# A fixed order for VectorE and ScalarE in the last stage of a fused kernel, block sums kept in DRAM, and the last tile product by product

## The chip, the cores and the metric

The kernel runs on one core of one Trainium2 chip. The metric is the device time of one execution in microseconds. Before the change it is 856.98 us, the median of three runs (856.64, 856.98 and 858.51).

## The reference

Windowed attention feeds two feed-forward blocks. The weights (w1, w2, w3, both w_out, w_in) are 64-bit floats, q, k and v are 32-bit, and the output is 32-bit.

```python
# attention: batch 4, heads 8, sequence 576, head size 64, window 64
scores = (q @ k.T) / 8, masked to 0 <= i - j < 64
x = softmax(scores) @ v                      # reshaped to 2304 tokens x 512
# first block: 512 -> 1024 -> 512
y = ((x @ w1) * (x @ w2)) @ w3 @ w_out
# second block: 512 -> 2048 -> 512
h = y @ w_in
g = maximum(0.01 * h, h)
out = (g @ w_out2).astype(float32)
```

## The kernel before, in words

Every matrix product is made of three products of split operands (`mm3`, lines 74 to 77): an operand is cut into a high part (a ScalarE copy to fp32r) and a low part (a VectorE subtraction), and high x high, high x low and low x high are added up in PSUM. So each operand tile costs one ScalarE and one VectorE pass before TensorE can use it; this is called a split below. 64-bit weights are loaded as words and made into 32-bit floats by integer operations (scale, shift, sign).

The work has four stages.

1. Weight words are loaded and converted, w3 and w_out are multiplied into one matrix, and the attention of batch 0 runs.
2. For each batch, `ab_step` and `y_step` compute (x w1)(x w2) and its product with w3 w_out, and store y to the DRAM tensor `yd`. The attention of the next batch and the words of w_in are woven in. In this attention p, the softmax result, is transposed by a store to DRAM (`pd`, line 213) and four loads back (`pts`, line 216).
3. h = y w_in by seven products of half-size blocks in place of eight (a Strassen form): 24 `Quad`s, one for each pair of column blocks p (0 to 7) and token group c (0 to 2), each of seven products of six matmuls. One product is one slot. `prepare(t)` runs what is planned for slot t: splits of y and w_in blocks with the sums that the form needs (`y_parts`, `w_parts`), the conversion of w_out2 words (`c_load`, `c_scale`, `c_shift`, `c_sign`, which end with a store to `wd`), and the first preparations of the last stage. h goes to DRAM (`hd`). c11, c21, c22, c12 (tiles `c`) collect the products; a ScalarE copy keeps a product, a VectorE add joins another (line 651).
4. out = g w_out2, again by seven products. A step is (g, k): a token group g of 512 tokens (the fifth has 256) and a pair k of blocks of w_out2, eight k to a group. For each step `h_load` fetches h, `h_sums` applies the leaky ReLU on ScalarE (line 814) and makes block sums on VectorE (lines 817 to 819), `h_split` makes the operand (lines 828 and 829), and `o_quad` runs 21 matmuls for each tile of 128 rows: two tiles to a step, one in group five. The operand of w_out2, one unit for each k, is made once by `v_load` (two loads from `wd`) and `v_parts`: four sums (line 788) and four splits (lines 791 and 792). After k = 7 `o_out` adds the seven products of a tile (lines 858 and 860) and stores two pieces of the output.

What sets the order: a scheduler places the instructions of each engine in a list before the run, from the program order, priorities (`first()`), and `tc.issue_after(x)`, which puts an instruction behind x in its list. At run time each engine works its list in order. DMAs issued by SyncE stand in one such list (SP) too. Pools with a number of buffers (raw 4, f 4, io 2, c 8) make a load or an operation wait until a buffer's last reader is done. The eight PSUM banks of the last stage (`ps3`) take the place of the eight of the stage before, and one tile of the output uses four of them through its eight k.

The order of the last stage before is this loop (line 974 on), whose instructions the scheduler may move against one another:

```python
h_load(i + 4); h_sums(i + 3)
for q in range(width(i) // P):
    o_quad(i, q)
h_split(i + 2)
if i < len(later): ...   # units 5 to 7 of w_out2
```

Of the kernel before, what the change touches and what calls it, by code (L numbers as in the profile page):

```python
# [21 lines left out]
def tile_kernel(ctx: ExitStack, tc: tile.TileContext, q, k, v, w1, w2, w3, w_out, w_in, w_out2, out):  # L22
# [62 lines left out]
    wd = dram.tile([2 * KF2, P, UC], F32, name="wd")  # L85

# [120 lines left out]
    def tp(g):  # L207
# [372 lines left out]
    def w_parts(p):  # L580
# [179 lines left out]
    def c_sign(f):  # L760
        u = conv.pop(f)
        g = u["f"].bitcast(I32)
        dve.scalar_tensor_tensor(out=g, in0=u["hi"], scalar=-0x80000000, in1=g, op0=ALU.bitwise_and, op1=ALU.bitwise_or)
        sp.dma_start(wd[KF2 + f], u["f"])

    vin, vop = {}, {}

    def v_load(k):
        vin[k] = stage.tile([P, 2, 2, 2 * P], F32, name="raw", tag="raw", bufs=RAW)
        for h in range(2):  # L770
            sp.dma_start(vin[k][:, h].rearrange("p c m -> p (c m)"), wd[KF2 + 2 * k + h])

    def v_parts(k, tile):

        own = {}

        def part(j):
            if j == 0:
                vop[k] = tile()
            u, t = vin[k], vop[k]  # L780
            a11, a21, a12, a22 = u[:, 0, 0], u[:, 0, 1], u[:, 1, 0], u[:, 1, 1]
            if j == 1:
                own["sums"] = [stage.tile([P, 2, 2 * P], F32, name="io", tag="io", bufs=2) for _ in range(2)]
            if j in (1, 2):
                s1, s2, s3, s4 = (own["sums"][i // 2][:, i % 2] for i in range(4))
                for o, x0, x1, op in (((s1, a21, a22, ALU.add), (s2, s1, a11, ALU.subtract)),
                                      ((s3, a11, a21, ALU.subtract), (s4, a12, s2, ALU.subtract)))[j - 1]:
                    dve.tensor_tensor(out=o, in0=x0, in1=x1, op=op)
            for at, x in (((0, u[:, 0, 0:1]), (1, u[:, 1])), ((3, own.get("sums", (0,))[0]),), ((5, own.get("sums", (0, 0))[-1]),))[j]:
                w = slice(at, at + x.shape[1])  # L790
                act.copy(t[:, 0, w], x)
                dve.tensor_tensor(out=t[:, 1, w], in0=x, in1=f32(t[:, 0, w]), op=ALU.subtract)
# [17 lines left out]
    def h_sums(i):  # L810

        if i < len(steps):
            x = hin[i]
            act.activation(out=x, in_=x, func=AF.Prelu, alpha=0.01)
            x = hin[i] = x.rearrange("p f (t m) -> p (f t) m", t=2)
            t13, t24 = hsum[i] = [stage.tile([P, 2, width(i)], F32, name="f", tag="f", bufs=4) for _ in range(2)]
            dve.tensor_tensor(out=t13, in0=x[:, 1:4:2], in1=x[:, 0:2], op=ALU.subtract)
            dve.tensor_tensor(out=t24[:, 0], in0=x[:, 3], in1=t13[:, 0], op=ALU.subtract)
            dve.tensor_tensor(out=t24[:, 1], in0=x[:, 2], in1=t24[:, 0], op=ALU.subtract)

    def h_split(i):

        if i < len(steps):
            x, (t13, t24) = hin.pop(i), hsum.pop(i)
            u = g_units[i % len(g_units)] if len(g_units) == 3 else g_units[i]
            for at, y in ((0, x[:, 0:1]), (1, x[:, 2:4]), (3, t13), (5, t24)):
                h, l = (u[:, n, at:at + y.shape[1], 0:width(i)] for n in range(2))
                act.copy(h, y)  # L828
                dve.tensor_tensor(out=l, in0=y, in1=f32(h), op=ALU.subtract)  # L829
# [3 lines left out]
    def o_quad(i, q):  # L833

        g, k = steps[i]
        w, y = vop[k], g_units[i % 3]
        ts = slice(P * q, P * q + P)
        if k == 0:
            po[g, q] = [ps3.tile([P, 2, 2 * P], F32, name="o") for _ in BANKS]
        for bank, ms in enumerate(BANKS):  # L840
            for n, m in enumerate(ms):
                a, b = O_PRODUCTS[m]
                with tc.issue_after(pss["pr"]):
                    pss["pr"] = mm3(po[g, q][bank][:, n], y[:, 0, b, ts], y[:, 1, b, ts], w[:, 0, a], w[:, 1, a],
                                    k == 0 and n == 0, k == NF - 1, True)
# [174 lines left out]
```

## Time and profile before

| | before |
|---|---|
| median of three runs | 856.98 us |
| the profiled execution | 859.36 us |
| its span, first to last instruction | 857.6 us |
| TensorE matmul busy | 806.6 us, 94% |
| VectorE busy | 583.9 us, 68% |
| ScalarE busy | 446.6 us, 52% |
| mean granted TensorE clock | 0.986 of full speed |

Busy shares are means over four unlike stages. What a change of one stage can be worth is read from TensorE's idle time and granted clock in that stage, and from what ended the idle time. Stage three runs from about 475 to 657 us of the span, stage four from there to the end.

### The profile page before, as it was taken

What the parts mean: (1) busy time and instruction counts of PE and PEld (TensorE: products, weight loads), DVE (VectorE), ACT (ScalarE), POOL (GpSimd) and SP (SyncE); (2) the same over time, 40 slices, a digit from 0 to 9 for tenths busy, and PEclk for the clock granted to TensorE, in tenths of its full rate; (3) what the DMA queues carried; (4) which work ended last, traced back from release to release, by engine and by line L of the source; (5) the groups of instructions that cost most, each with busy time, mean ns of one, the idle gap of its engine ahead of it and who ended that gap; (6) DMA issues with size and microseconds to landing.
All of it is one profiled execution on the core that took longest, in us unless ns stands there. A gap on an engine that the chain in (4) does not pass through costs nothing.

```text
span 857.6 us, 16756 instructions
## 1 busy us (share of the span) xinstructions
PE 806.6 (94%) x5980; PEld 774.5 (90%) x5980; DVE 583.9 (68%) x1505; ACT 446.6 (52%) x1095; POOL 66.4 (8%) x77
## 2 busy tenths in 40 slices
PE   5689799999999999898999999999998989999997
PEld 3567698999999999898999989999998988999997
DVE  6799896663655367665821765866569997788875
ACT  6687883432434244343521654655457675656543
POOL 1012553110111011110000000000000000000000
PEclk9999999999999999999999999999999999999999
DMA  7798688664545537667510346888756444343321
GB/s 244 202 221 221 190 213 203 145 145 89 126 109 135 114 98 179 181 182 236 182 46 2 111 157 233 296 286 278 246 184 203 133 150 131 115 144 104 124 86 63
DMA packets 200755, 139.52 MB, mean 163 GB/s; under 512 B 136416, under 2 KB 170720, under 8 KB 200672
## 3 DMA queue, kind: packets, MB, share of 16 engines
q1 hardware_dynamic: 196064, 133.74, 54.5%
q10 hardware_dynamic: 4608, 4.72, 1.7%
q8 instruction: 47, 0.77, 0.4%
q14 instruction: 36, 0.29, 0.1%
HBM read 94.63 MB, written 43.78 MB: 161 GB/s over the span
## 4 chain that ended last, share of the span: by engine, by line
PE 72%; DMA 10%; DVE 9%; ACT 3%; SPq 2%; issue 2%; POOL 0%; DVEq 0%; ACTq 0%; POOLq 0%
PE o L75 7%; PE o L77 7%; PE o L76 7%; PE ab L75 7%; PE ab L77 6%; PE ab L76 6%; PE pr L77 6%; PE pr L75 6%; PE pr L76 6%; PE mm L75 4%; DMA raw<-in_moe_w_dram 4%; PE mm L76 4%; PE mm L77 3%; PE sc L175 3%; PE pa L229 2%
## 5 line engine op out<-in xcount | busy, mean ns | idle before, releaser
L75 PE MATMUL ab<-x,w 128*128 128x288 f32 x512 | 154.2, 302 | 6.0 <-ACT x L235 2.8
L77 PE MATMUL ab<-x,w 128*128 128x288 f32 x512 | 152.1, 297 | 0.0
L76 PE MATMUL ab<-x,w 128*128 128x288 f32 x512 | 152.1, 297 | 0.0
L77 PE MATMUL pr<-yop,w 128*128 128x384 f32 x300 | 102.0, 340 | 2.5 <-DVE w L598 2.5
L75 PEld LDWEIGHTS ab<-x,w 128*128 128x128 f32 x512 | 97.2, 190 | 7.7 <-ACT x L235 2.9
L75 PE MATMUL pr<-yop,w 128*128 128x384 f32 x300 | 101.7, 339 | 0.0
L76 PE MATMUL pr<-yop,w 128*128 128x384 f32 x300 | 101.5, 338 | 0.0
L77 PEld LDWEIGHTS ab<-x,w 128*128 128x128 f32 x512 | 97.1, 190 | 0.1
L76 PEld LDWEIGHTS ab<-x,w 128*128 128x128 f32 x512 | 97.0, 190 | 0.1
L648 ACT COPY c<-pr 128x384 f32<-128x384 f32 x95 | 45.5, 479 | 67.1 <-PE pr L77 64.7
L75 PE MATMUL mm<-ab,wf 128*128 128x288 f32 x256 | 77.2, 313 | 2.1 <-ACT io L521 2.1
L75 PE MATMUL o<-yop,yop 128*128 128x256 f32 x259 | 74.4, 287 | 4.7 <-DVE res L858 3.0
L77 PE MATMUL mm<-ab,wf 128*128 128x288 f32 x256 | 74.8, 294 | 0.0
L76 PE MATMUL mm<-ab,wf 128*128 128x288 f32 x256 | 74.7, 294 | 0.0
L77 PE MATMUL o<-yop,yop 128*128 128x256 f32 x259 | 73.6, 284 | 0.0
L76 PE MATMUL o<-yop,yop 128*128 128x256 f32 x259 | 73.5, 284 | 0.0
L502 DVE TENSOR_TENSOR p<-ab,a 128x288 f32<-128x288 f32 x64 | 28.9, 452 | 60.5 <-PE ab L77 59.9
L651 DVE TENSOR_TENSOR c<-pr,c 128x384 f32<-128x384 f32 x74 | 41.1, 556 | 38.7 <-PE pr L77 22.0
L183 ACT ACTIVATE s<-s,nm 128x128 f32<-128x128 f32 x144 | 56.6, 396 | 20.0 <-DVE nm L179 19.2
L497 ACT COPY a<-ab 128x288 f32<-128x288 f32 x64 | 25.4, 398 | 77.9 <-PE ab L77 75.4
L829 DVE TENSOR_TENSOR yop<-f,yop 128x512 fp32r<-128x512 f32 (+1 forms) x80 | 48.7, 636 | 25.0 <-ACT yop L828 23.8
L192 POOL TENSOR_TENSOR s<-s,rs 128x384 f32<-128x384 f32 x48 | 41.3, 861 | 297.1 <-DVE rs L191 200.9
(127 smaller groups left out, 2095.7 us busy)
## 6 DMA issues: line engine op xcount, KB each, us to landing
hd<-c SPq DMA_DIRECT2D x96, 192.0 KB, 2.6
raw<-in_moe_w_dram SPq DMA_DIRECT2D x32, 512.0 KB, 4.7
raw<-hd SPq DMA_DIRECT2D x32, 512.0 KB, 3.7
raw<-in_moe_w_out_dram SPq DMA_DIRECT2D x24, 512.0 KB, 4.5
raw<-in_moe_w_in_dram SPq DMA_DIRECT2D x16, 512.0 KB, 4.9
wd<-f SPq DMA_DIRECT2D x32, 256.0 KB, 4.3
raw<-wd SPq DMA_DIRECT2D x30, 256.0 KB, 4.0
vt<-in_v_dram SPq DMA_DIRECT2D x56, 128.0 KB, 2.9
```

Of the source, the lines that this page charges most:

```text
L75: pe.matmul(ps, lhsT=lh, rhs=rh, start=first, stop=False, skip_group_check=more)
L76: pe.matmul(ps, lhsT=lh, rhs=rl, start=False, stop=False, skip_group_check=more)
L77: return pe.matmul(ps, lhsT=ll, rhs=rh, start=False, stop=last, skip_group_check=more).ins
L175: pe.matmul(sc[:, t, :], lhsT=qb[:, t, :], rhs=kT[n][:, k0:k0 + P], start=True, stop=True)
L183: act.activation(out=s[:, t, :], in_=s[:, t, :], func=AF.Exp, bias=nm[:, t:t + 1], scale=-1.0, accum_out=sm[:, t:t + 1])
L192: pool.tensor_tensor(out=s, in0=s, in1=rs.unsqueeze(2).to_broadcast([P, GT, P]), op=ALU.mult)
L229: pe.matmul(o[W * h:W * h + W, W * t:W * t + W], lhsT=vt[:, a, h, m, :], rhs=pts[:, 2 * h:2 * h + 2, t], start=True, stop=True)
L497: pss["copy"] = act.copy(pss["a"], ps).ins
L502: dve.tensor_tensor(out=p32, in0=ps, in1=pss["a"], op=ALU.mult)
L648: pss["copy"] = act.copy(self.sb[to], ps).ins
L651: pss["add"] = dve.tensor_tensor(out=self.sb[to], in0=self.ps[at], in1=self.sb[of or to], op=ALU.add).ins
L829: dve.tensor_tensor(out=l, in0=y, in1=f32(h), op=ALU.subtract)
```

## The change

- **Words behind p's store.** The loads of w_in's words in the second stage were issued behind the last of p's loads back (`pss["store"]` set at line 216); now behind p's store.
- **Buffers of `w_parts`' sums.** They were in io; now in raw for p = 1 and 2, in io for p = 0, in f for the rest.
- **Block sums of w_out2 in DRAM.** The words are converted in pairs, every 11 slots, and the four sums of a pair are made right after (`c_sums`) and stored to a new DRAM tensor `vd`. `v_load` loads them (two loads more, into f or io), and `v_parts` has splits only.
- **Fixed order of the last stage.** Every VectorE operation of it is tied behind the one before it in the program (`two`), every ScalarE operation too (`copy`, `split`); the first ones come behind the last add and the last copy of stage three. The loop has h_split(i + 2), h_sums(i + 3), units of w_out2, the products, then `o_out`; in a step with k = 7 h_sums comes after `o_out`.
- **The last tile product by product.** The last two k of the last tile are joined: product m of k = 6, then product m of k = 7, then the next m. Its last store is cut in two halves of columns, one issued by ScalarE.

```diff
-        sp.dma_start(pd, tb)
+        pss["store"] = sp.dma_start(pd, tb).ins
...
-            pss["store"] = sp.dma_start(pts[32 * b:32 * b + 32], pd[:, b].rearrange("(a j) t i -> j a (t i)", a=4)).ins
+            sp.dma_start(pts[32 * b:32 * b + 32], pd[:, b].rearrange("(a j) t i -> j a (t i)", a=4))
...
             if j == 1:
-                own["sums"] = [stage.tile([P, 2, 2, P], F32, name="io", tag="io", bufs=2) for _ in range(2)]
+                if p in (1, 2):
+                    both = stage.tile([P, 2, 2, 2, P], F32, name="raw", tag="raw", bufs=RAW)
+                    own["sums"] = [both[:, 0], both[:, 1]]
+                else:
+                    tag, n = ("f", 4) if p else ("io", 2)
+                    own["sums"] = [stage.tile([P, 2, 2, P], F32, name=tag, tag=tag, bufs=n) for _ in range(2)]
...
+    def c_sums(k):
+        f0, f1 = (conv.pop(2 * k + h)["f"] for h in range(2))
+        a11, a21, a12, a22 = (f[:, 2 * P * c:2 * P * c + 2 * P] for f in (f0, f1) for c in range(2))
+        sums = [stage.tile([P, 2, 2 * P], F32, name="io", tag="io", bufs=2) for _ in range(2)]
+        s1, s2, s3, s4 = (sums[i // 2][:, i % 2] for i in range(4))
+        for o, x0, x1, op in ((s1, a21, a22, ALU.add), (s2, s1, a11, ALU.subtract), (s3, a11, a21, ALU.subtract),
+                              (s4, a12, s2, ALU.subtract)):
+            dve.tensor_tensor(out=o, in0=x0, in1=x1, op=op)
+        for i in range(2):
+            sp.dma_start(vd[k, i], sums[i].rearrange("p c m -> p (c m)"))
+
+    chain = {}
+
+    def tied(name, f):
+
+        with tc.issue_after(chain[name]) if name in chain else nullcontext():
+            chain[name] = f().ins
...
+    def split(t, at, x, n):
+        h, l = (t[:, i, at:at + x.shape[1], 0:n] for i in range(2))
+        copy(h, x)
+        two(l, x, f32(h))
...
+        for h in range(2):
+            sp.dma_start(vin[k][1 + h].rearrange("p c m -> p (c m)"), vd[k, h])
...
-            if j in (1, 2):
-                s1, s2, s3, s4 = (own["sums"][i // 2][:, i % 2] for i in range(4))
...
+            u, s12, s34 = vin[k]
+            for at, x in (((0, u[:, 0, 0:1]), (1, u[:, 1])), ((3, s12),), ((5, s34),))[j]:
+                split(vop[k], at, x, 2 * P)
...
-    for f in range(KF2):
-        t0 = 38 + 5 * f
-        for n, g in ((0, c_load), (7, c_scale), (8, c_shift), (9, c_sign)):
-            at_slot(t0 + n, lambda f=f, g=g: g(f))
+    for k in range(NF):
+        t0 = 38 + 11 * k
+        for n, g, h in ((0, c_load, 0), (0, c_load, 1), (7, c_scale, 0), (8, c_shift, 0), (8, c_scale, 1), (9, c_sign, 0),
+                        (9, c_shift, 1), (10, c_sign, 1)):
+            at_slot(t0 + n, lambda f=2 * k + h, g=g: g(f))
+        at_slot(t0 + 11, lambda k=k: c_sums(k))
...
+    end = [(len(GROUPS) - 1, NF - 2), (len(GROUPS) - 1, NF - 1)]
+    for i, (g, k) in enumerate(steps):
+        with tc.issue_after(pss["copy"]), tc.issue_after(pss["add"]):
+            if i == 0:
+                h_sums(2)
+            h_load(i + 4)
+            h_split(i + 2)
+            if k < NF - 1:
+                h_sums(i + 3)
+            if i < len(later):
+                if i in (2, 4):
+                    v_load(5 + i // 2)
+                run(later[i])
+            for q in range(width(i) // P):
+                if (g, k) not in end:
+                    o_quad(g, q, [k])
+                elif k == NF - 1:
+                    o_quad(g, q, [k - 1, k])
+                if k == NF - 1:
+                    o_out(g, q)
+            if k == NF - 1:
+                h_sums(i + 3)
```

The lists of the two kernels differ on VectorE at these places. The first is the start of stage three, in the list before: w_6153 is the operand of w_in block p = 2, io_6165 and io_6166 its sums, raw_6209 and yop1_6185 belong to y of token group 1, and the c rows are adds that join products.

```order
L593 TENSOR_TENSOR io_6165<-raw_5981 128x256
L550 TENSOR_TENSOR raw_6210<-f_6035,f_6031 128x384
L550 TENSOR_TENSOR raw_6209<-f_6035,raw_6209 128x384
...
L598 TENSOR_TENSOR w_6153<-io_6165,w_6153 128x512
L553 TENSOR_TENSOR yop1_6185<-f_6254,yop1_6185 128x384
L553 TENSOR_TENSOR yop1_6185<-raw_6210,yop1_6185 128x384
L651 TENSOR_TENSOR c_6309<-pr_6314,c_6309 128x384
L550 TENSOR_TENSOR raw_6297<-f_6252,f_6250 128x384
L550 TENSOR_TENSOR raw_6298<-f_6256,f_6252 128x384
L553 TENSOR_TENSOR yop1_6185<-f_6256,yop1_6185 128x384
L598 TENSOR_TENSOR w_6153<-io_6166,w_6153 128x512
```

The same place in the list after, where the sums of p = 2 are in raw_6165 (those of p = 1 stand 25 rows further up, ahead of the last products of stage two).

```order
L657 TENSOR_TENSOR c_6151<-pr_6156,c_6151 128x384
L599 TENSOR_TENSOR raw_6165<-raw_5982 128x256 x2
L604 TENSOR_TENSOR w_6153<-raw_5982,w_6153 128x256
L599 TENSOR_TENSOR raw_6165<-raw_6165,raw_5982 128x256
L599 TENSOR_TENSOR raw_6165<-raw_5982,raw_6165 128x256
L604 TENSOR_TENSOR w_6153<-raw_5982,w_6153 128x512
L554 TENSOR_TENSOR yop1_6184<-f_6030,yop1_6184 128x384
L554 TENSOR_TENSOR yop1_6184<-f_6034,yop1_6184 128x384
L604 TENSOR_TENSOR w_6153<-raw_6165,w_6153 128x512 x2
L657 TENSOR_TENSOR c_6202<-pr_6187,c_6202 128x384
```

In the whole lists six adds of stage three stand ahead of the last split of p = 2 before, and one after; y's rows come behind it now.

The second place is the end of stage three on VectorE, in the list before. c_8041 is the last add; raw_8073 and raw_8078 are h of the steps 2 and 3, and io_8018 a sum of w_out2's unit 4.

```order
L651 TENSOR_TENSOR c_8043<-pr_8009,c_8041 128x384
L651 TENSOR_TENSOR c_8002<-pr_8046,c_8002 128x384
L818 TENSOR_TENSOR f_8083<-raw_8073,f_8082 128x256
L817 TENSOR_TENSOR f_8090<-raw_8078 128x512
L788 TENSOR_TENSOR io_8018<-raw_7923,io_8017 128x256
L829 TENSOR_TENSOR yop2_8080<-raw_8073,yop2_8080 128x256
L651 TENSOR_TENSOR c_8041<-pr_8055,c_8041 128x384
```

After, with c_8094 as the last add and raw_8133 as h of step 2:

```order
L794 TENSOR_TENSOR w_8063<-f_7982,w_8063 128x512
L657 TENSOR_TENSOR c_8096<-pr_8068,c_8094 128x384
L657 TENSOR_TENSOR c_8061<-pr_8099,c_8061 128x384
L657 TENSOR_TENSOR c_8094<-pr_8108,c_8094 128x384
L794 TENSOR_TENSOR f_8139<-raw_8133 128x512
L794 TENSOR_TENSOR f_8140<-raw_8133,f_8139 128x256
```

The sums of steps 2 and 3 stood ahead of the last add and now stand behind it.

The third place is the end of the first token group on VectorE, in the list before. The o tiles are the PSUM banks that `o_out` reads (first tile o_8095 to o_8098), the yop and f rows are splits and sums of later steps.

```order
L829 TENSOR_TENSOR yop_7632<-raw_8424,yop_7632 128x512
L858 TENSOR_TENSOR res_8579<-o_8095,c_8580 128x256
L858 TENSOR_TENSOR c_8581<-o_8096,c_8580 128x256
L819 TENSOR_TENSOR f_8554<-raw_8492,f_8554 128x256
L818 TENSOR_TENSOR f_8638<-raw_8550,f_8637 128x256
L829 TENSOR_TENSOR yop1_7863<-raw_8492,yop1_7863 128x256
L858 TENSOR_TENSOR c_8582<-o_8096,c_8581 128x256
L858 TENSOR_TENSOR res_8613<-o_8120,c_8614 128x256
L858 TENSOR_TENSOR c_8615<-o_8121,c_8614 128x256
L819 TENSOR_TENSOR f_8638<-raw_8550,f_8638 128x256
L829 TENSOR_TENSOR yop1_7863<-f_8553,yop1_7863 128x512
L858 TENSOR_TENSOR c_8581<-o_8097,c_8581 128x256
```

After, with the first tile in o_8165 to o_8168:

```order
L794 TENSOR_TENSOR yop_7703<-f_8551,yop_7703 128x512
L794 TENSOR_TENSOR res_8628<-o_8165,c_8629 128x256
L794 TENSOR_TENSOR c_8630<-o_8166,c_8629 128x256
L794 TENSOR_TENSOR c_8631<-o_8166,c_8630 128x256
L794 TENSOR_TENSOR c_8630<-o_8167,c_8630 128x256
L794 TENSOR_TENSOR res_8628<-o_8167,c_8631 128x2x256
L794 TENSOR_TENSOR res_8628<-o_8168,c_8630 128x256
L794 TENSOR_TENSOR res_8662<-o_8190,c_8663 128x256
```

Splits and sums stood between the reads of the banks; now the six reads of a tile stand together.

## Rows read from the trace of the kernel before

**Rows 1.** The page, part 1: span.

```profile
span 857.6 us, 16756 instructions
```

**Rows 2.** Stretches: length; busy (instructions) of PE, PEld, DVE, ACT, POOL; clock; DMA share, GB/s.

```profile
485.00:500.00 15.00, 12.51 (x61) 11.54 (x60) 13.87 (x30) 8.69 (x19) 0.00 (x0) 0.89 0.59 190
500.00:657.30 157.30, 157.30 (x900) 156.99 (x899) 106.64 (x212) 87.96 (x180) 0.00 (x0) 1.00 0.72 242
657.30:667.00 9.70, 6.41 (x40) 6.21 (x40) 7.99 (x18) 5.90 (x10) 0.00 (x0) 0.82 0.59 183
...
680.00:700.00 20.00, 20.00 (x171) 20.00 (x170) 20.00 (x43) 14.31 (x25) 0.00 (x0) 1.00 0.50 160
...
702.00:715.00 13.00, 9.01 (x55) 8.06 (x54) 11.20 (x27) 6.72 (x12) 0.00 (x0) 0.87 0.48 162
...
751.50:756.00 4.50, 3.82 (x27) 3.05 (x26) 4.50 (x12) 1.14 (x3) 0.00 (x0) 1.00 0.63 189
...
798.00:852.84 54.84, 54.84 (x461) 54.63 (x459) 37.58 (x100) 27.24 (x63) 0.00 (x0) 1.00 0.25 78
```

**Rows 3.** Waits of PE from 474.8 us on: total us, times, longest.

```profile
PE pr L77 <- DVE w L598: 2.5, 2, 2.1
...
PE o L75 <- DVE res L858: 3.5, 4, 1.5
PE o L75 <- DVE c L651: 3.3, 2, 2.6
```

**Rows 4.** Timeline, start of stage three: start, length, operation, [idle before <- releaser].

```profile
480.79 0.43 DVE L593 TENSOR_TENSOR io<-raw 128x256 f32<-128x256 f32 x1 [1.39 <-ACT w L597]
...
495.84 0.69 DVE L598 TENSOR_TENSOR w<-io,w 128x512 fp32r<-128x512 f32 x1
...
496.58 0.69 PE L77 MATMUL pr<-yop,w 128*128 128x384 f32 x1 [2.08 <-DVE w L598]
```

**Rows 5.** Timeline, from stage three to four.

```profile
659.32 1.06 ACT L814 ACTIVATE raw<-raw 128x1024 f32<-128x1024 f32 x1 [3.58 <-DMA raw<-hd]
...
660.40 0.69 DVE L817 TENSOR_TENSOR f<-raw 128x512 f32<-128x512 f32 x1 [1.71 <-ACT raw L814]
...
661.68 0.55 DVE L651 TENSOR_TENSOR c<-pr,c 128x384 f32<-128x384 f32 x1
...
662.29 0.38 PE L75 MATMUL o<-yop 128*128 128x256 f32 x1 [2.65 <-DVE c L651]
```

**Rows 6.** One stretch, line 788 alone: length, DVE busy (instructions), clock, DMA.

```profile
641.00:695.00 54.00, 9.69 (x24) 0.97 0.51 161
```

**Rows 7.** Timeline, end of the second token group.

```profile
753.13 0.42 DVE L858 TENSOR_TENSOR res<-o,c 128x256 f32<-128x256 f32 x1
...
753.60 0.39 PE L75 MATMUL o<-yop,yop 128*128 128x256 f32 x1 [0.56 <-DVE res L858]
```

**Rows 8.** Timeline, the end.

```profile
852.56 0.28 PE L77 MATMUL o<-yop,yop 128*128 128x256 f32 x1
...
853.18 1.01 DVE L858 TENSOR_TENSOR res<-o,c 128x512 f32<-128x512 f32 x2
...
854.31 0.39 SPq L870 DMA_DIRECT2D out_dram<-res  x1
```

**Rows 9.** Timeline, p's round trip late in stage two.

```profile
385.51 0.42 SPq L213 DMA_DIRECT2D pd<-tb  x1
...
391.22 1.74 SPq L216 DMA_DIRECT2D pts<-pd  x4
...
394.67 0.57 PE L229 MATMUL pa<-pts,vt 128*64 128x64 f32 x12 [2.03 <-DMA pts<-pd]
```

**Rows 10.** DMA issues, 360 to 400 us, and whole page: count, KB, us to landing.

```profile
raw<-in_moe_w_in_dram SPq DMA_DIRECT2D x8, 512.0 KB, 4.8
...
pts<-pd SPq DMA_DIRECT2D x20, 48.0 KB, 1.9
...
wd<-f SPq DMA_DIRECT2D x32, 256.0 KB, 4.3
```

More of the change, by code (lines that the diff above doesn't have):

```diff
@@ L85, in tile_kernel @@
     wd = dram.tile([2 * KF2, P, UC], F32, name="wd")
+    vd = dram.tile([NF, 2, P, UC], F32, name="vd")
     stage = tc.alloc_tile_pool(name="stage", bufs=2, side="right")
@@ L764, in c_sign, with copy, two @@
         sp.dma_start(wd[KF2 + f], u["f"])
+    def c_sums(k):
[12 more added lines that the diff above has]
+            chain[name] = f().ins
+    def copy(out, x):
+        tied("act", lambda: act.copy(out, x))
+    def two(out, in0, in1, op=ALU.subtract):
+        tied("dve", lambda: dve.tensor_tensor(out=out, in0=in0, in1=in1, op=op))
+    def split(t, at, x, n):
+        h, l = (t[:, i, at:at + x.shape[1], 0:n] for i in range(2))
+        copy(h, x)
+        two(l, x, f32(h))
     vin, vop = {}, {}
     def v_load(k):
-        vin[k] = stage.tile([P, 2, 2, 2 * P], F32, name="raw", tag="raw", bufs=RAW)
+        tag, n = ("f", 4) if k in (0, 2, 4) else ("io", 2)
+        u = stage.tile([P, 2, 2, 2 * P], F32, name="raw", tag="raw", bufs=RAW)
+        vin[k] = [u] + [stage.tile([P, 2, 2 * P], F32, name=tag, tag=tag, bufs=n) for _ in range(2)]
         for h in range(2):
-            sp.dma_start(vin[k][:, h].rearrange("p c m -> p (c m)"), wd[KF2 + 2 * k + h])
+            sp.dma_start(u[:, h].rearrange("p c m -> p (c m)"), wd[KF2 + 2 * k + h])
+        for h in range(2):
+            sp.dma_start(vin[k][1 + h].rearrange("p c m -> p (c m)"), vd[k, h])
     def v_parts(k, tile):
-        own = {}
         def part(j):
@@ L842, in o_quad @@
                 a, b = O_PRODUCTS[m]
-                with tc.issue_after(pss["pr"]):
-                    pss["pr"] = mm3(po[g, q][bank][:, n], y[:, 0, b, ts], y[:, 1, b, ts], w[:, 0, a], w[:, 1, a],
-                                    k == 0 and n == 0, k == NF - 1, True)
-        if k == NF - 1:
-            with first():
-                o_out(g, q)
+                for k in ks:
+                    w, y = vop[k], g_units[(g * NF + k) % 3]
+                    with tc.issue_after(pss["pr"]):
+                        pss["pr"] = mm3(po[g, q][bank][:, n], y[:, 0, b, ts], y[:, 1, b, ts], w[:, 0, a], w[:, 1, a],
+                                        k == 0 and n == 0, k == NF - 1, True)
     def o_out(g, q):
@@ L855, in o_out @@
         lo, hi = slice(0, 2 * P), slice(2 * P, 4 * P)
[L857 to L865 removed]
+        copy(own, m1)
+        two(res[:, 0, lo], m2, own, ALU.add)
+        two(u2, m6, own, ALU.add)
+        two(u3, m7, u2, ALU.add)
+        two(u2, m45[:, 1], u2, ALU.add)
+        two(res[:, :, hi], m45, u3.unsqueeze(1).to_broadcast([P, 2, 2 * P]), ALU.add)
         r0 = GROUPS[g][0] + P * q
         r1 = r0 + GROUPS[g][1] // 2
+        end = g == len(GROUPS) - 1
         sp.dma_start(out[r0:r0 + P, :], res[:, 0])
[L869 to L870 removed]
+        if end:
+            act.dma_start(out[r1:r1 + P, hi], res[:, 1, hi])
+        two(res[:, 1, lo], m3, u2, ALU.add)
+        cols = lo if end else slice(0, DM)
+        sp.dma_start(out[r1:r1 + P, cols], res[:, 1, cols])
     FIRST = 3
@@ L970, in tile_kernel @@
         later += [(a,), (b, c)]
+    v_load(5)
     h_load(2)
-    v_load(5)
     h_load(3)
-    for i in range(len(steps)):
-        if i == 0:
-            three(ph, "yop2")
-            g_units.append(spare.pop())
-            h_sums(2)
-        h_load(i + 4)
-        h_sums(i + 3)
-        for q in range(width(i) // P):
-            o_quad(i, q)
-        h_split(i + 2)
-        if i < len(later):
-            if i % 2 == 0 and i:
-                v_load(5 + i // 2)
-            run(later[i])
+    three(ph, "yop2")
+    g_units.append(spare.pop())
+    end = [(len(GROUPS) - 1, NF - 2), (len(GROUPS) - 1, NF - 1)]
[20 more added lines that the diff above has]
+                h_sums(i + 3)
     for p in (ps3, po_out, yb0, ph, stage):
```

45 lines of the change are left out of this document (10 added, 35 removed).

## The prediction, made before the changed kernel was timed

> **What bounds the kernel now.** The page gives a span of 857.6 us [rows 1]. I read the stretches first [rows 2]: their first column pair is TensorE's busy time with its matmuls, the one before the DMA share the granted clock. From 500 to 657.3 us TensorE is busy for all of 157.30 us; 900 matmuls there make 0.175 us each, so a product of six, one slot, is 1.05 us. From 798 us to the last matmul it is busy too; 461 in 54.84 us make 0.119 us. A two-tile step of the last stage, 42 matmuls, is therefore 5.0 us. Where matmuls follow each other at these paces, nothing that another engine saves moves the end. So the question is what is lost against the paces, and where:
>
> - 485 to 500 us: 61 matmuls need 10.7 of 15.0 us, 4.3 are lost;
> - 657.3 to 667: 40 need 4.8 of 9.7, 4.9 are lost;
> - 702 to 715: 55 need 6.5 of 13.0, 6.5 are lost;
> - 751.5 to 756: 27 need 3.2 of 4.5, 1.3 are lost; the end of the next token group (from 793) repeats it, so 2.6 in both.
>
> That makes 18.3 us. Only part of each loss is waiting. The mean clock is 0.89, 0.82 and 0.87 in the first three stretches [rows 2]: after a wait TensorE goes on for some time at 1.2 in place of 2.4 GHz. A removed wait gives both back.
>
> Next the waits of TensorE [rows 3], all on VectorE: for `w` (2.5 us), for the last add of stage three (3.3) and for `o_out` (the res row's 3.5). VectorE is full there: 43 operations fill all 20 us from 680 to 700 us [rows 2], 0.465 us each. So in this stretch two things count, how much VectorE does and what stands ahead of the operation that TensorE waits for.
>
> **The change part by part.** Durations are from the execution profiled, 859.36 us; it lies 2.38 above the median, and the sum is brought there at the end.
>
> *Start of stage three.* VectorE stands 1.39 us idle, then makes the first of p = 1's sums in io at 480.79; the last split of p = 2 starts at 495.84 and TensorE waits 2.08 us for it [rows 4]. After the change the sums have raw, those of p = 1 are made while stage two still runs, and p = 2's last split has one add ahead of it, not six. What is late next is y of token group 1, which now comes behind, with loads that stand in SP's list behind stores of c as before. TensorE reaches that group 21 slots (22 us) into the stage, so I take 4.0 of the 4.3 us. Bounds: 0, if y takes the wait over, and 4.3.
>
> *From stage three to four.* TensorE waits 2.65 us for the add at 661.68. It is in VectorE's list behind a sum (line 817, 660.40) that waits for a ReLU, which waits 3.58 us for h from DRAM [rows 5]. After, no operation of the last stage stands ahead of the last add. I take 4.6 of 4.9 us, since the first bank still waits for an add after the last product but two; bounds 3.3 (the listed waits alone, the clock low for another reason) and 4.9.
>
> *The steps 0 to 5.* Two steps hold 8 splits, 6 sums, and a unit of w_out2 with 4 splits and 4 sums: 22 operations, at 0.465 us 10.2 us against TensorE's 10.0. VectorE can't keep up, and falls back by what it brings along from stage three. The sums of the units go: 24 of the 32 lie between 641 and 695 us and cost 9.69 us [rows 6]. Then 18 operations are left, 8.5 us of 10.0. At k = 7 `o_out`'s twelve operations, about 5 us, come on top, with the banks now read in one piece: splits of a step first, about 2 us, then tile 1, then tile 2. TensorE needs tile 1's first bank one step, 5.0 us, after k = 7 began, and it is read after about 3. I take 6.3 of 6.5 us; bounds 3 (VectorE's lead lost to late h loads) and 6.5.
>
> *The other group ends.* At 753.13 a res add frees the bank that TensorE has waited 0.56 us for, behind splits and sums of later steps [rows 7]. By the count above none stands there now: 2.6, bounds 0 and 2.6.
>
> *Words behind p's store.* A store of p issued at 385.51 us is waited for until 391.22, when its four loads go out, and TensorE waits 2.03 us for them [rows 9]. The store came late and slowly, since SP had sent two loads of words just ahead of it, which had waited behind the loads of the p before. After, words go out while p's store is on its way, and the next store finds the queue emptier. I take 2.0; bounds +4 (a loss: the words hold up p's loads, see the rivals) and -2.0.
>
> *The last tile.* The last matmul ends at 852.84; behind it come a c add and two res adds to 854.19, and the last store goes out at 854.31 [rows 8]. Product by product, six matmuls in place of three follow the last read of that c add, 0.36 us more cover, and half of the last store goes earlier on another queue. I take 0.5; bounds 0 and 1.0.
>
> *What it adds.* 32 sums in stage three at 0.40 us (9.69 / 24), 13 us of VectorE where it is busy for 106.64 of 157.30 us: hidden on the mean. 16 stores and 16 loads of 256 KB, issued by SP among stores of c. The words come in pairs: the second `c_scale` waits for the one `low` buffer, which VectorE frees in the first `c_shift`, and ScalarE's copies of products stand behind that. Before, the two halves were five slots apart. No row shows this wait. From below it costs nothing, as VectorE has 50 us spare; from above each of the eight pairs costs TensorE a wait like that for `w`, 2.08 us, 16 in all. I take 1.5, nearer to nothing, as before no wait of stage three past 500 us came from the conversion at all.
>
> Sum: 4.0 + 4.6 + 6.3 + 2.6 + 2.0 + 0.5 - 1.5 = 18.5. 859.36 - 18.5 = 840.9 in an execution like the one profiled; minus 2.38, 838.5 us.
>
> **The rivals.**
>
> *The last stage is bound by loads, not by VectorE.* The ReLU's 3.58 us for h [rows 5] is a DMA wait, and a unit of w_out2 now takes four loads. If h and the units come late, the fixed order passes each delay on to all that follows, where the scheduler's order let other work through. Against it: h is loaded further ahead in SP's list, and an operand is due two steps, 10 us, after its split begins. It would leave the 4.6 and half of the 6.3: 838.5 + 7.8, about 846.
>
> *Words hold up p's loads.* A load of words takes 4.8 us to land, p's loads 1.9 [rows 10]. Now each of about ten stands ahead of p's loads. In these rows the wait for p's store covers most of a load of words; if not, p's loads come up to 2.9 us later, and some of ten make TensorE wait. Without the 2.0, and with 4 lost: 844.5. The Trainium skill says in "DMA: Bandwidth & Descriptors", section "Queues, rings and completion order", that each DMA engine takes the descriptors of a ring in order, so that p's small loads would stand behind the words whole. By that alone each pair would add the 2.9 us; the row at 391.22, with p's loads sent 5.7 us after the store, says that most of it is over by then, and no run so far shows the new order.
>
> *Stage three stalls: slower.* Its place is the conversion. A pair's two f buffers come free when its sums are made and its last store has landed, 4.3 us [rows 10], four slots, after slot 10 or 11 of the pair; the next pair takes f in slot 18, and `w_parts` of p = 3 to 7 take two f in between. The margin is three slots, 3.1 us. If SP's or VectorE's list is later than that, ScalarE stands at `c_scale`, copies stop, and TensorE, without a wait there now, waits at half clock after. It decides from a loss of 2.5 us a pair on (20.0 / 8): 3 us in eight pairs make 857.0 - 20.0 + 24, some 861. Against it: 157.30 of 157.30 us busy today with the same buffers.
>
> *The change does not act.* The lists after show that it does; what could still undo it is a loss elsewhere of just its size: 857.
>
> **How the numbers follow.** Forecast 0.61, with its own range 833.5 to 843; load-bound 0.16; words 0.08; no change 0.06; slower 0.09. The first three are faster by more than 0.2% (1.7 us, what a measurement can tell from no change): 0.85. The range runs from 833.5, where every bound is met (21.3 in all: 835.7) and the runs' spread of 1.9 helps too, to 848.5, which takes in the first two rivals and leaves the rest out.
>
> **What would show it.** In the profile after: no wait of TensorE for w near 495 us, nor for c near 655; a stretch from 655 to 690 us at 0.119 us a matmul and clock 1.00; VectorE idle for a tenth or more in the steps 0 to 5; no wait for res at the group ends; p's loads landing before TensorE wants them; some 4 us from last matmul to end. Wrong it would be if 500 to 650 us shows waits of TensorE for ScalarE's copies, if the waits at the start of the last stage are for splits with h from DRAM behind, or if yop1 takes the place of w.

## The result and the profile after

The changed kernel takes 834.43 us (median of 4 runs, 832.89 to 835.99), the kernel before in the same runs 857.75 (856.64 to 858.72). The ratio is 0.9729, 95% interval 0.9705 to 0.9752. The execution profiled of the changed kernel took 834.71 us, with a span of 832.9 against 857.6 [rows 1].

Where the 24.7 us of the spans come from is read from four points that both traces have: the start of the matmuls of the values near 284 us (their fifteenth group from the end), the first product of stage three, the first of the last stage, and the end of the last matmul. The table gives the stretches between them, for all kernels of this document, from the start of those rows in each trace:

| kernel | before the values' matmul | to stage three | stage three | last stage | last matmul to end |
|---|---|---|---|---|---|
| before | 284.84 | 191.31 | 181.80 | 194.89 | 4.76 |
| after | 284.91 | 185.18 | 178.29 | 180.48 | 4.04 |
| after, second time | 282.02 | 185.16 | 177.63 | 180.48 | 4.01 |
| words only | 283.68 | 185.17 | 180.42 | 193.57 | 4.66 |
| words earlier still | 280.91 | 188.13 | 180.42 | 196.63 | 4.71 |
| all but words | 283.25 | 194.94 | 181.18 | 180.49 | 4.04 |
| order without kept sums | 280.76 | 185.64 | 177.57 | 194.68 | 4.05 |
| kept sums without order | 281.35 | 185.17 | 180.22 | 187.05 | 4.01 |
| old tail | 280.00 | 185.29 | 178.97 | 180.49 | 4.75 |
| w's sums in io | 284.50 | 185.17 | 181.83 | 180.48 | 4.02 |
| w spread | 282.20 | 185.18 | 178.16 | 180.49 | 4.07 |
| w spread, loaded early | 279.57 | 185.23 | 176.37 | 180.49 | 4.04 |

From before to after: 6.1 us ahead of stage three, 3.5 in it, 14.4 in the last stage, 0.7 at the end. The first column, which no edit touches, moves by 5 us from execution to execution. So an effect of 1 or 2 us is read from the other columns, not from a median. These too are steady only where TensorE has no wait: the last stage takes 180.48 or 180.49 us in the seven rows of the table in which it runs without one, but the old last stage, the same in three kernels, takes 193.57, 194.89 and 196.63, and the old stage three 180.42 in two of them and 181.80 in the third.

The stretches of the kernel after at the places of [rows 2], columns as there:

```profile
479.00:494.00 15.00, 15.00 (x87) 15.00 (x86) 13.02 (x28) 8.59 (x19) 0.00 (x0) 1.00 0.68 223
494.00:648.00 154.00, 153.59 (x878) 152.92 (x877) 110.56 (x225) 87.57 (x180) 0.00 (x0) 1.00 0.86 290
648.30:658.00 9.70, 9.70 (x83) 9.70 (x82) 9.28 (x18) 8.70 (x16) 0.00 (x0) 1.00 0.70 239
671.00:691.00 20.00, 20.00 (x170) 20.00 (x169) 18.51 (x39) 12.43 (x24) 0.00 (x0) 1.00 0.52 173
692.00:705.00 13.00, 13.00 (x111) 13.00 (x111) 12.53 (x26) 10.14 (x17) 0.00 (x0) 1.00 0.49 155
741.50:746.00 4.50, 4.50 (x40) 4.50 (x39) 4.39 (x9) 3.14 (x6) 0.00 (x0) 1.00 0.40 121
```

TensorE is busy throughout in all but the second, at clock 1.00. At the border of the stages it does 83 matmuls in 9.70 us where it did 40, at the first group's end 111 in 13.00 where it did 55. VectorE has 1.5 of 20 us free where it had none.

All of TensorE's waits after 300 us, in one row (total us, times, longest), against the list in [rows 3]:

```profile
PE pr L75 <- ACT c L654: 1.2, 2, 0.8
```

Both are new, and both stand in stage three. The timeline shows ScalarE at the first, then ScalarE and TensorE at the second (start, length, operation, idle before it and who ended it):

```profile
470.77 1.97 ACT L603 CAST w<-raw 128x256 fp32r<-128x256 f32 x4 [0.58 <-ACT io L522]
472.64 0.47 ACT L654 COPY c<-pr 128x384 f32<-128x384 f32 x1
...
545.41 0.41 ACT L603 CAST w<-raw 128x256 fp32r<-128x256 f32 x1 [1.51 <-DMA raw<-wd]
545.72 0.47 ACT L654 COPY c<-pr 128x384 f32<-128x384 f32 x1
...
546.25 0.44 PE L75 MATMUL pr<-yop,w 128*128 128x384 f32 x1 [0.41 <-ACT c L654]
```

At 470.77 four splits of `w` are made ahead of the first copy of a product. At 545.41 a split has stood 1.51 us for its load, and the copy behind it stood too.

The border, VectorE alone, against [rows 5]: the last add is at once followed by the first sum of the last stage, which stood ahead of it before.

```profile
648.58 0.56 DVE L657 TENSOR_TENSOR c<-pr,c 128x384 f32<-128x384 f32 x1 [0.31 <-PE pr L77]
649.05 0.68 DVE L794 TENSOR_TENSOR f<-raw 128x512 f32<-128x512 f32 x1
```

The end, against [rows 8]: last matmul, last adds, and the three last stores, two of them issued at the same time on two queues.

```profile
828.53 1.01 DVE L794 TENSOR_TENSOR res<-o,c 128x512 f32<-128x512 f32 x2
828.58 0.28 PE L77 MATMUL o<-yop,yop 128*128 128x256 f32 x1
829.24 0.35 SPq L887 DMA_DIRECT2D out_dram<-res  x1
829.24 0.38 ACTq L889 DMA_DIRECT2D out_dram<-res  x1
829.68 0.38 SPq L892 DMA_DIRECT2D out_dram<-res  x1
```

### The profile page after: what moved, and what is told of

Its sections match the earlier page's. It is cut to its first block, busy times and chain, and to the rows that moved or that the text cites. A ratio compares the mean times of both kernels' runs of the same rounds, so it can differ in the third digit from the quotient of the medians.

```text
span 832.9 us, 16724 instructions
## 1 busy us (share of the span) xinstructions
PE 796.3 (96%) x5980; PEld 767.8 (92%) x5980; DVE 589.0 (71%) x1505; ACT 447.9 (54%) x1095; POOL 67.2 (8%) x77
## 4 chain that ended last, share of the span: by engine, by line
PE 79%; DMA 10%; DVE 4%; ACT 4%; issue 1%; SPq 1%; POOL 0%; DVEq 0%; ACTq 0%; POOLq 0%
PE o L76 7%; PE o L77 7%; PE o L75 7%; PE ab L75 7%; DMA raw<-in_moe_w_dram 7%; PE ab L77 7%; PE ab L76 7%; PE pr L75 7%; PE pr L77 7%; PE pr L76 7%; PE mm L75 4%; PE mm L76 4%; PE mm L77 4%; PE sc L176 3%; PE pa L230 2%; ACT f L299 1%
## 5 line engine op out<-in xcount | busy, mean ns | idle before, releaser
L76 PE MATMUL o<-yop,yop 128*128 128x256 f32 x259 | 73.0, 282 | 0.0
L77 PE MATMUL o<-yop,yop 128*128 128x256 f32 x259 | 72.9, 282 | 0.0
L75 PE MATMUL o<-yop,yop 128*128 128x256 f32 x259 | 72.9, 281 | 0.0
L791 ACT CAST yop<-raw 128x256 fp32r<-128x256 f32 (+1 forms) x92 | 42.5, 485 | 35.6 <-PE o L76 34.8
```

The costliest lines, as they stand in the source:

```text
L75: pe.matmul(ps, lhsT=lh, rhs=rh, start=first, stop=False, skip_group_check=more)
L76: pe.matmul(ps, lhsT=lh, rhs=rl, start=False, stop=False, skip_group_check=more)
L77: return pe.matmul(ps, lhsT=ll, rhs=rh, start=False, stop=last, skip_group_check=more).ins
L791: tied("act", lambda: act.copy(out, x))
```

## The experiments

### Words: alone, left out, and one step earlier

The surprise was the 6.1 us ahead of stage three. The trace of before, read again there, has more than the wait in [rows 9]. ScalarE and TensorE in the kernel before:

```profile
363.30 0.66 ACT L298 ACTIVATE f<-raw 128x512 f32<-128x512 f32 x1 [3.91 <-DMA raw<-in_moe_w_in_dram]
363.86 0.38 ACT L521 COPY io<-mm 128x288 f32<-128x288 f32 x1
...
364.29 0.40 PE L75 MATMUL mm<-ab,wf 128*128 128x288 f32 x1 [2.06 <-ACT io L521]
...
388.50 0.66 ACT L298 ACTIVATE f<-raw 128x512 f32<-128x512 f32 x1 [3.56 <-DMA raw<-in_moe_w_in_dram]
```

ScalarE stands 3.91 us at the conversion of words that have not landed. The copy of a finished product stands behind it, and TensorE waits 2.06 us for the copy's bank. At 388.50 ScalarE has stood 3.56 us for words once more; VectorE's next step of the conversion waits for it, the product of (x w1) and (x w2) stands behind that step in VectorE's list, and TensorE waits 0.72 us for it at 390.78. Three ways to place the words followed; the first on the kernel before, the second on the kernel after in reverse, the third on before:

```
words only                              words earlier still
-    sp.dma_start(pd, tb)               -    dve.transpose(out=tb..., in_=s...)
+    pss["store"] = sp.dma_start(pd,    +    pss["store"] = dve.transpose(out=tb...,
+        tb).ins                        +        in_=s...).ins
-        pss["store"] = sp.dma_start(   -        pss["store"] = sp.dma_start(
-            pts[...], pd[...]).ins     -            pts[...], pd[...]).ins
+        sp.dma_start(pts[...], ...)    +        sp.dma_start(pts[...], ...)
```

> The kernel before, with the one edit that loads of words now follow p's store and not p's last load. Theory A (late words: ScalarE stands at a conversion of words that have not landed, and copies that TensorE wants stand behind it): all 5.5 us of TensorE's waits between 348 and 393 us go and what the low clock adds to them, so about 6 us: 851.7 us, with the first product of stage three at about 470 us in place of 476.15. Theory B (the prediction's sum, only p's own round trip gets shorter): 2.0 us, 855.7. Theory C (words hold up p's loads): no gain, 857.7 or more, with waits of TensorE for pts.

Measured, words only: 849.33 us (846.85 to 856.25, 7 runs), ratio 0.9907, 0.9867 to 0.9946. The stretch ahead of stage three is 185.17 us, as in the kernel after, with no wait of TensorE of 0.25 us or more from 340 us to its end. Theory A's size holds, B and C fall.

> The kernel after, with loads of words again behind p's last load; all else of the change stays. Theory A (late words block ScalarE): the 6 us come back, 840.5 us, first product of stage three near 476 us, and again a wait of ScalarE of some 3.5 us for words near 363 and 388 us. Theory B (prediction's sum): 836.4. Theory C (words hold up p's loads): 834.4 or less.

Measured, all but words: 841.72 us (839.22 to 845.70), ratio 0.9794, 0.9745 to 0.9842. The stretch is 194.94 us, longer even than before. TensorE's waits from 300 us on:

```profile
PE pa L230 <- DMA pts<-pd: 3.6, 2, 1.8
PE pr L75 <- ACT c L654: 2.8, 2, 2.0
PE mm L75 <- ACT io L522: 2.4, 1, 2.4
```

The first and the last are the two kinds of wait of before. Both belong to late words; with the words moved both go. They add up to 6.0 us, hardly more than the 5.5 of before. Most of the 3.6 us by which the stretch is longer than in before goes with TensorE's clock: from 363 to 373 and from 393 to 403 us it is 0.83, where before has 1.00 from 365 to 375 and from 395 to 405 (the last section has rows of it). So the edit was worth 6.1 us with the clock up, and 9.8 (194.94 - 185.18) with it down.

> The kernel before, with loads of words following the transpose ahead of p's store, one step earlier than in the first run: in SP's list some of them now stand right ahead of a store of p, others behind it, none behind the wait for that store. Theory A (ScalarE stands at late words): stage two is as short as in the first run, 185.2 us from the matmul of the values that starts near 284 us to stage three, against 191.3 of before; 0.991 of before or a little less. Theory B (the prediction's: p's store comes late and slowly behind words): TensorE waits about 2 us for pts at one or more places after 340 us, and of the 6.1 us at most 4 are gained.

Measured, words earlier still: 853.01 us (849.30 to 856.40, 10 runs), ratio 0.9919, 0.9892 to 0.9947. ScalarE waits for no words any more, yet the stretch is 188.13 us: 3.2 of the 6.1 gained. SP and TensorE of this kernel at its longest wait:

```profile
335.57 0.43 SPq L279 DMA_DIRECT2D raw<-in_moe_w_in_dram  x1
336.04 0.47 SPq L387 DMA_DIRECT2D wd<-f  x1
336.61 0.38 SPq L213 DMA_DIRECT2D pd<-tb  x1
337.09 0.44 SPq L279 DMA_DIRECT2D raw<-in_moe_w_in_dram  x1
337.58 0.61 SPq L387 DMA_DIRECT2D wd<-f  x1
341.42 2.82 SPq L216 DMA_DIRECT2D pts<-pd  x4
...
345.83 0.36 PE L229 MATMUL pa<-pts,vt 128*64 128x64 f32 x5 [1.61 <-DVE rs L191]
```

p's store at 336.61 stands behind words, its loads go out 4.8 us later, and TensorE's matmul on `pts` starts some 1.6 us after the last of them was issued. The profile names VectorE's `rs` as the releaser, which that matmul does not read; I take it for the late `pts`, since the wait in [rows 9], put down to `pts`, also ends 1.7 us after the last load was issued. Two more waits at `pts` are 0.15 and 0.17 us. The rest of the 3 us is not p's: at 360.32 TensorE waits 0.55 us for ScalarE, which has stood 3.13 us until a store of y landed. So theory B is right in part: p's store behind words costs about 2 us here. The DMA issues from 340 to 400 us show it: p's loads and its store (count, KB each, median us to landing), in the kernels before, after, and words earlier still:

```profile
pts<-pd SPq DMA_DIRECT2D x28, 48.0 KB, 1.9
pd<-tb SPq DMA_DIRECT2D x6, 192.0 KB, 4.4
```

```profile
pts<-pd SPq DMA_DIRECT2D x28, 48.0 KB, 2.6
pd<-tb SPq DMA_DIRECT2D x6, 192.0 KB, 2.7
```

```profile
pts<-pd SPq DMA_DIRECT2D x28, 48.0 KB, 2.3
pd<-tb SPq DMA_DIRECT2D x6, 192.0 KB, 4.3
```

With the words between store and loads, the store lands in 2.7 us and not 4.4, the loads take 0.7 longer. SP waits for the store 22.8, 10.9 and 19.6 us in the three, seven times each. So the 6.1 us are two costs of one fault: ScalarE standing at late words, and p's store slowed by words ahead of it. By the four waits of before they are about half each: 2.06 and 0.72 us behind ScalarE, 2.03 and 0.67 at matmuls on `pts`. The 0.67, at 348.83, is put down to a VectorE product that its matmul does not read; the last of p's loads had been issued 1.6 us before.

### The last stage: order alone, kept sums alone

Both start from the kernel after. "Order without kept sums" makes the four sums of a unit in the last stage, in the fixed order in front of the unit's splits. "Kept sums without order" takes the ties away and writes the loop as it was.

```
 order without kept sums                     kept sums without order
     u, s12, s34 = vin[k]                     def tied(name, f):
+    if j:                                   -    with tc.issue_after(chain[name]) ...:
+        for o, x0, x1, op in (...)[j - 1]:  -        chain[name] = f().ins
+            two(o, x0, x1, op)              +    f()
     (no vd, no c_sums)                       (loop: h_sums, o_quad, o_out first, h_split)
```

> The kernel after, but the block sums of w_out2 are made in the last stage again (four operations a unit, in the fixed order, in front of the unit's splits), and neither made in stage three nor kept in DRAM. Theory D (VectorE's count of work in the first steps of the last stage): 24 sums by 0.40 us come back there, 9.7 us, and VectorE has 2 to 3 us free between 648 and 700 us, so TensorE loses some 6.5 us: 841, with waits for splits between 655 and 700 us. Theory E (the order alone did it): 834.4 to 835.5, no wait past 650 us; stage three gains at most 1 us from the work taken out.

> The kernel after, but the operations of the last stage are not tied to each other, nor to the copies and adds of stage three, and stand in the code in the old order, o_out with high priority; the sums kept in DRAM and the joined last tile stay. Theory E (order): the loss at the border of stages three and four (4.6) and that at the group ends (2.6) come back, 841.6 us, with TensorE waiting for c near 655 us and for res at a group's end. Theory D (count of VectorE's work): VectorE has room, the waits stay away but for the last add's, 834.4 to 837.

Measured: 844.52 us (843.79 to 847.33), ratio 0.9828, 0.9791 to 0.9865, and 840.99 us (839.62 to 844.49), ratio 0.9787, 0.9746 to 0.9828. In the table the order alone leaves the last stage at 194.68 us, the sums alone bring it to 187.05, both to 180.48. What is lost against 0.1195 us a matmul, summed from start to start of TensorE's rows, by place:

| last stage | border | first steps and first group's end | later group ends |
|---|---|---|---|
| before | 4.5 | 6.7 | 3.2 |
| order alone | 0.8 | 13.3 | 0.1 |
| kept sums alone | 0.1 | 3.2 | 3.3 |
| both | 0.1 | 0.0 | 0.0 |

A wait ahead of the last stage's first matmul comes on top, counted in stage three: 0.64, 0, 1.14 and 0 us in this order. (The order alone has a wait of 0.50 us for the last add too, but 2.1 us behind that matmul, within its 0.8.)

So each part does something of its own. Later group ends are a matter of order alone. At the border either takes most of the loss: 5.1 us before, wait included, 0.8 with the order, 1.2 with the sums. The first group's end needs both: the kept sums alone halve its loss, the order alone leaves it (6.7 of the 13.3), and loses 6.6 more in the steps ahead of it, where before and the kept sums alone lose nothing. TensorE's waits (order alone, from 640 us):

```profile
PE o L75 <- ACT yop L783: 3.3, 4, 1.2
PE o L77 <- DVE yop L786: 1.5, 4, 0.5
PE o L75 <- DVE res L786: 1.0, 2, 0.7
PE o L76 <- DVE yop L786: 0.7, 2, 0.3
PE o L75 <- DVE c L656: 0.5, 1, 0.5
```

Theory E, the order alone, falls. Theory D gave the right sign and half the size (6.5 us expected, 14.2 lost), and its reason is not the whole one: VectorE (third pair of columns) is not full in this stretch of some seven steps:

```profile
644.00:694.00 50.00, 44.05 (x317) 41.25 (x316) 43.64 (x87) 30.00 (x55) 0.00 (x0) 0.94 0.44 132
```

It has 6.4 of 50 us free, and TensorE falls behind all the same. VectorE and then ScalarE of this kernel in one unit:

```profile
674.86 0.42 DVE L786 TENSOR_TENSOR io<-io,raw 128x256 f32<-128x256 f32 x1
675.97 0.69 DVE L786 TENSOR_TENSOR yop<-io,yop 128x512 fp32r<-128x512 f32 x1 [0.69 <-ACT yop L783]
```

```profile
675.32 0.62 ACT L783 CAST yop<-io 128x512 fp32r<-128x512 f32 x1 [3.42 <-DVE io L786]
677.37 0.62 ACT L783 CAST yop<-io 128x512 fp32r<-128x512 f32 x1 [1.43 <-DVE io L786]
```

In a fixed order ScalarE stands for a sum of VectorE (3.42, then 1.43 us) and VectorE for ScalarE's copy of it (0.69 us), twice a unit. Sums that come from DRAM need neither. These rows are the evidence for this cause; no run changed the hand-over alone. In the run without order the wait at the border is a single one, ahead of the last stage's first matmul, and the group ends show again:

```profile
PE o L75 <- DVE res L793: 2.3, 4, 0.9
PE o L75 <- DVE c L657: 1.1, 1, 1.1
PE o L75 <- DVE c L793: 0.8, 1, 0.8
```

Theory E forecast this run's time (841.6), though not its places: it put 4.6 us at the border, where 1.2 were lost, and 2.6 at group ends, where 6.5 were.

### The start of stage three

```
-                if p in (1, 2):
-                    both = stage.tile([P, 2, 2, 2, P], F32, name="raw", tag="raw", bufs=RAW)
-                    own["sums"] = [both[:, 0], both[:, 1]]
-                else: tag, n = ("f", 4) if p else ("io", 2)
+                tag, n = ("f", 4) if p > 2 else ("io", 2)
...
```

> The kernel after, with the block sums of w of p = 1 and p = 2 in the two io buffers again (they are in raw in the kernel after); p = 3 to 7 keep f. Theory J (the prediction's first term): the sums of p = 1 wait for io until stage two's last stores have landed, all of VectorE's list shifts, and TensorE waits about 2.5 us for the last splits of w some 10 to 20 us into stage three, 4 us with the low clock: stage three takes about 181.5 us in place of 177.6 to 178.3, 1.005 of the kernel after. Rival K (the wait came from other work in VectorE's list, gone by now): stage three as in the kernel after.

Measured: 837.45 us (835.98 to 840.60), ratio 0.9740, 0.9686 to 0.9795. Stage three takes 181.83 us, 3.5 and 4.2 more than in the two profiles of the kernel after. The old wait is back, with its old size [rows 4]:

```profile
PE pr L77 <- DVE w L600: 2.5, 2, 2.1
```

Theory J holds.

### The last tile, and the two waits that are left

The next four kernels were timed in one set. The first is the kernel after once more, as the measure of the others.

> The kernel after once more, unchanged, as the measure for the next three. All theories: 0.973 of before, 834.4 us; TensorE waits in stage three for copies of products near 473 us (0.83 us) and 546 us (0.4 to 2.0 us), and nowhere from the start of the last stage on.

Measured: 831.54 us (830.86 to 833.36, 6 runs), ratio 0.9710, 0.9685 to 0.9735. The wait at the start of stage three is there again (0.82 us), the one near 546 us is not. Of the seven profiles of kernels that keep the sums in DRAM and load `w` as the kernel after does, six show it, with 0.41, 0.46, 1.25, 1.31, 1.62 and 1.98 us; so it changes from execution to execution, and is worth 0 to 2 us. The four profiles without kept sums (before, words only, words earlier still, order without kept sums) have no wait of TensorE at all from 500 to 643 us, so it goes with the kept sums. In the kernel after, SP issues the split's load at 540.46, right behind a store of such sums.

```
-                if (g, k) not in end: o_quad(g, q, [k])
-                elif k == NF - 1: o_quad(g, q, [k - 1, k])
+                o_quad(g, q, [k])
...
-        if end: act.dma_start(out[r1:r1 + P, hi], res[:, 1, hi])
...
-        sp.dma_start(out[r1:r1 + P, cols], res[:, 1, cols])
+        sp.dma_start(out[r1:r1 + P, :], res[:, 1])
```

> The kernel after, with the last tile's last two units of w_out2 one after the other again in place of product by product, and its last store undivided on one queue. Theory H (the prediction's last term): the last matmul to the end takes 0.5 us more (bounds 0 to 1.0) than the 4.0 of the kernel after, about 4.5; 834.9 us. Rival I (the end is set by the last store's landing alone, which stays one store behind the last add): no difference, 834.4.

Measured: 831.86 us (830.17 to 834.99), ratio 0.9717, 0.9687 to 0.9746. The times cannot tell this from the kernel after, the trace can: 4.75 us from the last matmul to the end, against 4.04 and 4.01. Theory H holds, with 0.7 in place of 0.5. The order of the products and the halved store were not tried apart.

```
 both                                        w spread, loaded early
-    run(w_parts(1))                         -   at_slot(t0 - 8, lambda p=p: w_load(p))
-    for n, f in enumerate(w_parts(2)):      +   at_slot(t0 - 12, lambda p=p: w_load(p))
+    for n, f in enumerate(w_parts(1) + w_parts(2)):
```

> The kernel after, with only the first half of the run before: parts of p = 1 in slots 0 to 3, of p = 2 in slots 4 to 7; loads of w stay. Theory F: the wait near 473 us goes, the one near 546 us stays, 833.4 us. Rival G (only the spread of p = 2's splits hurts): TensorE waits for w near 485 us as before the change, 2 us with the low clock twice that, 836 or more.

> The kernel after, with the parts of p = 1 in slots 0 to 3 of stage three and those of p = 2 in slots 4 to 7 (they were ahead of slot 0, and in 0 to 3), and with the loads of w of p = 3 to 7 issued four slots earlier. Theory F (the two waits left are ScalarE standing at, or busy with, a split of w in front of a copy of products): both go, 1.2 to 2.8 us and half as much again from the low clock: 832 us or 0.997 of the kernel after. Rival G (the earlier load takes one of the four raw buffers from the words of w_out2, and the splits of p = 2 come too late): new waits of TensorE, for w near 480 us or for copies between 500 and 645 us, 834.4 us or more.

Measured, spread alone: 831.82 us (829.86 to 832.60), ratio 0.9704, 0.9677 to 0.9731. The first wait is gone, the second is there with 1.62 us, and the medians cannot tell the kernel from the one after. With the early loads too: 829.36 us (827.50 to 829.65, 5 runs), ratio 0.9675, 0.9648 to 0.9701. No run of it is as slow as the fastest of the kernel after in the same set. Stage three takes 176.37 us, and TensorE has no gap after 300 us:

```profile
480.00:636.00 156.00, 156.00 (x894) 155.86 (x893) 114.91 (x235) 89.08 (x184) 0.00 (x0) 1.00 0.86 293
650.00:810.00 160.00, 160.00 (x1344) 160.00 (x1343) 139.36 (x292) 101.62 (x184) 0.00 (x0) 1.00 0.43 138
```

Theory F holds for the first wait. For the second it rests on the times, all under the fastest of the kernel with the late loads (829.86), more than on this one profile, since one profile of seven with late loads had no such wait either. This version beats both kernels, by 0.3% the one after (829.36 / 831.54 = 0.997).

## Why the prediction was right, and where it was not

The forecast was 838.5 us, range 833.5 to 848.5; 834.43 lies inside, at its lower end, and in part by luck: with every bound met the prediction's own sum reaches 835.7 us, and only the 1.9 us allowed below it for the runs' spread take 834.43 in. The second timing of the same kernel, 831.54 us where before took 857.93, lies under the range. The gain came at the places named, but one size was far off and some of the reasons held only in part. Against the execution profiled, 840.9 was forecast and 834.71 came: 6.2 us more gain. That the median came only 4.1 lower is due to the 2.38 us taken off for the execution; the kernel after's profiled one stands just 0.3 above its median.

- **Words behind p's store: the mis-sized term.** 2.0 was taken, with -2.0 as the lower bound; 6.1 was measured, by the edit alone as in the whole change, and 9.8 when it alone was taken back and the clock fell as well. The step that failed is in the prediction's words "TensorE waits 2.03 us for them": it priced one wait. It left out the other three waits of TensorE between 340 and 400 us, and did not look at ScalarE, which stood 3.91 us at one conversion in the same stretch. What it did price was real: words ahead of p's store cost 2 to 3 us. Two thirds of the miss, 4.1 of 6.2 us, are here.
- **Words hold up p's loads (rival).** It did not come. Loads land 0.7 us later, not 2.9, and SP's wait for the store falls from 22.8 to 10.9 us. The Trainium skill's rule in "DMA: Bandwidth & Descriptors", section "Queues, rings and completion order", on rings taken in order, had been read as 2.9 us for each pair; the loads show 0.7. With the stores this case's rows agree: one with words ahead of it takes 4.3 to 4.4 us, one without 2.7. They do not show whether order in a ring or the sharing of the DMA engines makes the difference.
- **Start of stage three.** 4.0 was taken, 3.5 to 4.2 measured by putting the sums back in io. The prediction's "A removed wait gives both back" holds only for some executions: before, words only and words earlier still have the same two waits of TensorE here (0.37 to 0.39 and 2.08 or 2.09 us), but the clock falls in before alone, and its stage three takes 181.80 us against 180.42 in both others. So 1.4 us of this term are not lost each time.
- **What it adds.** 1.5 was taken: a wait near 546 us of 0 to 2.0 us, and the 0.8 at 473 us, which the forecast did not have; that one is absent with the sums in io, so it belongs to the edit at the start of the stage. Without both, stage three is 1.9 us shorter than in the profile after. The cause near 546 us is not the one described (ScalarE at `c_scale` for `low`) but a split of `w` whose load landed late, in SP's list behind a store of kept sums. The slower rival, 3 us in each of eight pairs, did not come.
- **From stage three to four.** 4.6 of 4.9 was taken; 0.64 and 4.5 went. The reason given was the order; the runs show that the sums kept in DRAM alone also do most of it (1.2 us left).
- **Steps 0 to 5, first group's end.** 6.3 was taken, 6.7 measured, all of it at the group's end and none in the steps 1 to 6. The reason, 22 operations at 10.2 us against 10.0, was half of it: without kept sums a fixed order loses more than before while VectorE has 6 of 50 us free, and the rows of a unit show sum, copy and subtraction waiting for each other in turn.
- **Other group ends.** 2.6 was taken, 3.2 measured, and the order alone does it.
- **The last stage bound by loads (rival).** No wait of TensorE past 648 us, so nothing of it.
- **The last tile.** 0.5 was taken, 0.7 measured.

## What to carry to other kernels

A late load can cost more than the one wait that is seen first: before pricing a load that is moved, list what each of its readers does behind it, not only the wait that the bottleneck shows at one place. A fixed order of two engines pays little where an operation needs the one just ahead of it on the other engine; here order and less work gave 0 and 8 us of the last stage alone, 14 together. And effects of a few us are measured between fixed points of the trace, when an untouched first part moves by 5 us.

## What the runs showed of the hardware

- The same wait was followed by a low clock in one execution and not in another. At the start of stage three TensorE waits 2.08 us for `w` in before and in words only. In the next 3 us the granted clock is 0.50, which is the level of 1.2 GHz, in the first, and 1.00, 2.4 GHz, in the second (columns as in [rows 2]):

```profile
496.50:499.50 3.00, 2.92 (x9) 2.92 (x10) 2.37 (x6) 1.03 (x2) 0.00 (x0) 0.50 0.56 186
489.20:492.20 3.00, 2.94 (x17) 2.94 (x18) 3.00 (x8) 1.03 (x2) 0.00 (x0) 1.00 0.60 184
```

In stage two, behind the wait for `io` of 2.06 us in before and of 2.38 us in all but words, it is 1.00 and 0.65:

```profile
364.30:367.30 3.00, 3.00 (x29) 2.77 (x30) 2.97 (x12) 1.52 (x6) 0.00 (x0) 1.00 0.82 200
364.10:367.10 3.00, 2.97 (x15) 2.97 (x16) 2.97 (x12) 1.53 (x6) 0.00 (x0) 0.65 0.83 222
```

What decides it no run here shows. At the border too: after waits of 0.64 and 2.65 us it was 0.82 over 9.7 us in before [rows 2], with 4.5 us lost, and 1.00 for 6 us behind waits of 0.64 and 2.33 us in words earlier still, with 2.7 lost. After a single wait of 1.14 us (kept sums alone) the stretch from 645.6 to 657 us has 1.00 and loses 0.1 us more:

```profile
645.60:657.00 11.40, 10.26 (x86) 10.26 (x86) 11.40 (x24) 9.02 (x17) 0.00 (x0) 1.00 0.72 238
```

- ScalarE passed no copy ahead of a conversion that waited for its load (363.30 and 363.86 us above). The Trainium skill says in "PSUM — Partial Sum Buffer", section "Engine vs sequencer instructions", that ScalarE's queue is strictly first in, first out; these rows agree.
